# A gated recurrence with a convolutional gate on one core: tangents taken for each gate apart

## The chip, the cores and the metric

The kernel runs on one core of a Trainium2 chip. The core has a matrix engine (TensorE, PE in the profile, with its weight loads as PEld), a vector engine (VectorE, DVE), a scalar engine that evaluates functions from tables (ScalarE, ACT), a fourth engine for elementwise work (GpSimd, POOL), and a queue that issues transfers between the memory outside the core and the memory on it (SyncE, SP). The metric is the device time of one execution in microseconds (us). Where a time stands without more, it comes from the profiled execution.

## The reference: what is computed

There are three inputs of 4 sequences x 6336 steps x 256 channels in single precision: `x`, `r_gate` and `i_gate`. A gated linear recurrence runs along each sequence, and its output goes through a linear layer that is gated by a short causal convolution.

```
log_a = 8 * sigmoid(r_gate) * log(sigmoid(a_param))     # a_param: one number per channel
a     = exp(log_a)
u     = sqrt(max(1 - a*a, 1e-6)) * sigmoid(i_gate) * x
h[t]  = a[t] * h[t-1] + u[t]                            # along the sequence; y = h
gate  = sigmoid(sum over k of conv_w[k] * y[t-4+k])     # five taps, per channel, zeros ahead of the sequence
out   = (gate * (y @ w_val)) @ w_out                    # two 256 x 256 matrices
```

The steps `a*a`, the square root and the product with `i_gate` and `x` are independent of the recurrence, but the recurrence needs them; everything behind `y` needs the recurrence.

## The kernel before, in words

**Tiling.** The four sequences are laid end to end, 25344 rows. They are cut into 51 windows, 48 of 512 rows and 3 of 256 (windows 0, 1 and 50). The windows form 28 chunks: chunks 0, 1 and 27 are one short window each, chunks 2 and 26 one window of 512 each, and the 23 chunks between have two windows (chunk 3 is windows 3 and 4, chunk 4 windows 5 and 6, and so on). The chunks form 12 batches, mostly of three chunks; a batch shares one square root. Sigmoids are computed as tanh: sigmoid(z) = (1 + tanh(z/2)) / 2.

**Stages.** The kernel is a list of small operations. Their names are the words of a long string, `ORDER`, with the number of the window (w), chunk (c), half of the channels (h) or batch (b) that they work on:

- `lr.w`, `li.w`, `lx.w` (line 274): load r, i and x of a window, 512 KB for a window of 512 rows, issued by SP. `st.w` (line 493): store the output of a window, also issued by SP.
- `th.w` (line 289, ACT): the tanh of r and i of a window in one operation, 2048 elements in each partition for a window of 512 rows.
- `tr.c.h` (line 334, PE): transpose the tanh of r of a pair of chunks, so that time lies along the row. `ex.c.h` (line 350, ACT): the exponential, which gives a.
- `sq.c.h` (line 358, POOL): a*a; `sa.c.h` (line 366, ACT) is the same on ACT. `rt.b` (line 377, ACT): the square root for a batch. The exponential and the tanh are in one set of ACT's tables and the square root in another, so that a table load (line 509) stands ahead of rt and behind it.
- `pp.w` (line 297, POOL) adds one to the tanh of i, and `up.w` (line 309, POOL) multiplies with x, which gives u without its root. For a few windows `xp.w` (line 314, PE) and `uv.w` (line 323, DVE) do that in place of pp and up.
- `nt.c` (line 392, PE) transposes the root, `xg.c` (line 399, DVE) multiplies it into u, `xt.c` (line 408, PE) transposes u. `sc.c.h` (line 430, DVE): the recurrence, a scan.
- `cv.w` (line 442, PE): the convolution, as matmuls. `tg.w` (line 449, ACT): its tanh. `vl.w` (line 457, PE): y @ w_val. `gv.w` (line 462, DVE): gate times value. `ou.w` (line 472, PE): times w_out. `cd.w` (line 480, DVE) or `ca.w` (line 482, ACT): copy the result out of the matmul banks.

**What sets the order.** `ORDER` is written out in full. Each engine, and SP's queue, runs its own words in the order of the string, and waits for what it needs from another engine; a word that waits holds up every later word of its engine. The numbers behind an @ are the matmul banks that an operation uses.

**Rings.** Data between the stages lie in rings with a fixed number of places. r and i share one ring of 4 windows (`riring`). The tangents go to `tring`, with 3 windows of three planes each: the tanh of i is always in the middle plane, the tanh of r in the first or in the last in turn (`swapped`), so that one operation writes two planes that lie side by side:

Of the kernel before, what the change touches and what calls it, by code (L numbers as in the profile page):

```python
# [8 lines left out]
P = 128  # L9
CONV_K = 5  # L10
FP32 = mybir.dt.float32
BF16 = mybir.dt.bfloat16
# [12 lines left out]
NRI = 4  # L25
NX = 4
NTRI = 3
# [6 lines left out]
s_ident s_small s_kt s_diag li.2 lr.2 th.2 lr.3 lr.0 li.0 th.0 pp.0 tr.2.0@0 li.1 lr.1 tr.0.0@1 ex.2.0 th.1 lx.0 lx.2  # L34
li.3 up.0 tr.2.1@2 ex.2.1 tr.0.1@0 ex.0.0 tr.1.1@3 ex.1.1 tr.1.0@4 sq.1.1 ex.0.1 sq.0.1 lx.3 xp.3@0,1 lx.1 lr.6 th.3
sq.0.0 rt.0 lr.5 sq.2.0 pp.2 up.2 nt.0@5 xg.0 xt.0@2,3 li.5 th.5 sq.2.1 li.6 lr.4 uv.3 th.6 pp.6 pp.5 xp.1@5 sc.0.0
sc.0.1 cv.0@2,3 uv.1 li.4 th.4 tg.0 s_wl.1 ex.1.0 lx.4 li.7 tr.3.1@0,1 s_wl.0 lr.7 ex.3.1 lx.5 tr.3.0@2,3 ex.3.0
s_wl.3 lx.6 lx.7 pp.4 up.4 th.7 lr.9 rt.2 xp.7@2,3 li.8 uv.7 sa.4.0 sq.4.1 sq.3.1 sq.1.0 rt.1 nt.2@0 xg.2 nt.1@1 xg.1
s_wl.2 lr.8 li.10 lx.8 xt.2@2,3 xt.1@0,1 sc.1.1 li.9 lr.10 sq.3.0 rt.3 li.11 up.6 sc.1.0 lx.10 lr.11 sc.2.1 sc.2.0
up.5 th.8 lx.11 s_wcast th.10 lx.9 pp.10 up.10 lr.14 th.9 li.13 li.14 lr.13 xp.8@4,5 li.12 lr.12 uv.8 th.11 li.15  # L40
nt.3@0,1 xg.3 nt.4@6,7 pp.11 up.11 cv.1@2,3 tg.1 xg.4 xt.3@0,1 sc.3.1 vl.1@4,5 tr.5.0@6,7 ex.5.0 sq.5.0 tr.5.1@2,3
gv.1 ou.1.0@1 cd.1.0 st.1 lx.12 lr.15 ex.5.1 vl.0@4,5 xp.9@6,7 th.14 sq.5.1 cv.2@2,3 sc.3.0 th.13 uv.9 lx.13 xt.4@1,0
gv.0 ou.0.0@4 cd.0.0 st.0 sc.4.1 lx.15 cv.3@6,7 th.12 li.16 li.18 tr.7.1@4,5 tg.2 vl.2@2,3 gv.2 tg.3 ex.7.1 sq.6.1
sq.6.0 lx.14 pp.14 pp.12 up.12 tr.7.0@6,7 ex.7.0 sq.7.0 lx.16 cv.4@2,3 tg.4 th.15 ou.2.0@4,5 cd.2.0 sc.4.0 st.2 lr.18
lr.16 vl.3@6,7 xp.13@2,3 vl.4@4,5 gv.4 sq.7.1 rt.4 uv.13 th.16 sq.8.1 sq.8.0 pp.15 up.15 li.17 lr.17 up.14 ou.4.0@4,5
li.19 cv.5@0,1 lr.19 gv.3 cd.4.0 lx.17 tg.5 ou.3.0@6,7 lx.18 st.4 cd.3.0 st.3 nt.5@4,5 li.20 xg.5 pp.16 up.16 th.17
pp.17 lr.20 nt.7@6,7 xg.7 lx.19 li.21 nt.6@2,3 xg.6 th.18 pp.18 lr.21 xt.5@4,5 sc.5.1 up.17 vl.5@6,7 cv.6@0,1 tg.6
th.19 tr.9.1@2,3 ex.9.1 li.22 lr.22 up.18 sq.9.1 pp.19 gv.5 sc.5.0 tr.9.0@6,7 ex.9.0 lx.20 ou.5.0@0,1 cd.5.0 sq.10.1
xt.6@5,4 up.19 sc.6.1 cv.7@0,1 tg.7 cv.8@2,3 th.20 lr.24 tg.8 sc.6.0 vl.6@6,7 gv.6 xt.7@0,1 cv.9@4,5 ou.6.0@6,7 sc.7.0
th.21 tg.9 cd.6.0 vl.7@2,3 gv.7 vl.9@6,7 th.22 tr.11.0@0 sc.7.1 ou.7.0@2,3 vl.8@4,5 sq.9.0 tr.12.0@1 gv.9 ou.9.0@6,7  # L50
gv.8 ou.8.0@4,5 sq.10.0 st.5 cd.7.0 cd.9.0 lx.22 st.6 rt.5 lx.21 nt.8@6,7 lr.23 li.23 cd.8.0 nt.9@4,5 pp.22 pp.21
up.22 pp.20 up.20 up.21 xg.8 ex.12.0 xg.9 ex.11.0 li.24 st.7 st.9 li.25 lr.25 lx.23 lx.24 li.26 lr.26 th.23 xt.8@6,7
sc.8.0 sq.11.0 pp.23 sq.12.0 lr.27 li.27 cv.11@2,3 tg.11 cv.10@4,5 sc.8.1 cv.12@0,1 st.8 th.24 pp.24 tg.10 tg.12
vl.11@2,3 tr.11.1@6 ex.11.1 gv.11 vl.10@4,5 gv.10 th.25 xt.9@0,1 sc.9.0 tr.12.1@2 ex.12.1 ou.11.0@6,7 cd.11.0
ou.10.0@4,5 cd.10.0 cv.14@2,3 up.23 lx.25 lx.27 th.26 nt.10@6,7 sc.9.1 st.11 li.29 st.10 tg.14 tr.13.0@4,5 xg.10 up.24
sq.11.1 th.27 ex.13.0 tr.13.1@2,3 vl.12@0,1 gv.12 sq.12.1 li.30 lr.30 lx.26 pp.25 pp.27 sq.13.0 xt.10@6,7 sc.10.1
ex.13.1 sq.13.1 up.27 sq.14.0 pp.26 up.25 lr.28 cv.13@4,5 tg.13 vl.13@0,1 gv.13 li.28 vl.14@2,3 gv.14 ou.12.0@4,5
# [42 lines left out]
def kernel(  # L100
# [82 lines left out]
    with tc.manual_schedule():  # L183
# [357 lines left out]
```

## Time and profile before

| | |
|---|---|
| median of 3 runs | 301.36 us (300.97 to 302.71) |
| the profiled execution | 300.32 us, its span 298.5 us |
| ACT busy | 278.8 us (93%), 197 instructions |
| DVE busy | 247.6 us (83%), 206 instructions |
| PE busy | 246.4 us (83%), 2509 matmuls |
| POOL busy | 232.8 us (78%), 155 instructions |
| moved by transfers | 104.75 MB, 351 GB/s over the span |
| granted PE clock | 0.977 of full speed |

The span is the time from the first to the last instruction on the core; the device time is a little longer. The profile gives each engine's busy time; the same in 40 slices of the span, where a digit is the busy share in tenths; groups of instructions by line; who waited for whom; and the instructions in order of time, with their start, their duration and, in brackets, the idle time ahead of them and what ended it.

### The profile page before, as it was taken

To read this page: it belongs to the slowest core of one execution; us is meant where nothing else is said; L and a number is where in the kernel's file an instruction comes from. 1 tells how busy PE (TensorE), PEld (TensorE's weight loads), DVE (VectorE), ACT (ScalarE), POOL (GpSimd) and SP (SyncE) were. 2 spreads that over 40 slices of the span, in tenths; PEclk is the share of its full clock that TensorE was granted. 3 is DMA by queue.
4 is the path that set the end of the run, shared out by engine and by line. 5 is a ranking of instruction groups with operands and counts; after the bars stand their busy time and mean duration, and the time that the engine had idled before them with its cause. 6 is when DMAs were issued, how large, how long until landed. Compare 5 with 4: busy or idle time off the path is not lost.

```text
span 298.5 us, 6286 instructions
## 1 busy us (share of the span) xinstructions
PE 246.4 (83%) x2509; PEld 167.8 (56%) x2509; DVE 247.6 (83%) x206; ACT 278.8 (93%) x197; POOL 232.8 (78%) x155
## 2 busy tenths in 40 slices
PE   0374577897888598989898899998979999899993
PEld 0134255454556466757664758567647675666662
DVE  2030288849999889999999999999999899899993
ACT  6799999999999999999999999999999999969863
POOL 1478958989999899899999879998995996255300
PEclk9997599999999979999999999999999999999999
DMA  6999999999999999999999998999999977726046
GB/s 252 408 408 385 379 411 407 406 414 406 337 379 370 419 416 415 411 406 321 417 411 375 388 417 335 396 353 361 349 409 419 408 278 270 273 116 248 29 186 246
DMA packets 29995, 104.75 MB, mean 351 GB/s; under 512 B 3335, under 2 KB 3854, under 8 KB 29966
## 3 DMA queue, kind: packets, MB, share of 16 engines
q1 hardware_dynamic: 29952, 104.35, 90.5%
q8 instruction: 19, 0.31, 0.4%
q14 instruction: 10, 0.08, 0.1%
q10 hardware_dynamic: 14, 0.01, 0.0%
HBM read 78.39 MB, written 25.95 MB: 350 GB/s over the span
## 4 chain that ended last, share of the span: by engine, by line
ACT 31%; PE 23%; DVE 13%; issue 13%; DMA 12%; POOL 5%; SPq 1%; ACTq 0%; DVEq 0%; POOLq 0%
ACT tring L289 10%; ACT aring L350 8%; DMA riring<-in_r_gate_dram 7%; DVE yring L430 7%; PE banks L442 5%; ACT tgring L449 5%; PE banks L457 5%; ACT ering L377 4%; PE banks L472 4%; PE banks L392 3%; DMA riring<-in_i_gate_dram 3%; DVE tgring L462 3%; DVE oring L480 2%; DMA xring<-in_x_dram 2%; ACT L509 2%
## 5 line engine op out<-in xcount | busy, mean ns | idle before, releaser
L430 DVE TENSOR_TENSOR_SCAN yring<-aring,yring,banks 128x1024 bf16<-128x1024 f32 (+5 forms) x54 | 106.2, 1988 | 0.9 <-PE banks L408 0.6
L358 POOL TENSOR_TENSOR ering<-aring 128x1024 f32<-128x1024 f32 (+2 forms) x54 | 91.5, 1713 | 9.7 <-ACT aring L350 9.7
L309 POOL TENSOR_TENSOR uring<-tring,xring 128x1024 bf16<-128x1024 bf16 (+1 forms) x45 | 94.6, 2113 | 4.9 <-DMA xring<-in_x_dram 3.5
L289 ACT ACTIVATE tring<-riring 128x2048 bf16<-128x2048 f32 (+1 forms) x51 | 93.8, 1867 | 4.1 <-DMA riring<-in_i_gate_dram 1.9
L297 POOL TENSOR_SCALAR tring<-tring 128x1024 bf16<-128x1024 bf16 (+1 forms) x45 | 45.8, 1026 | 30.5 <-ACT tring L289 30.4
L442 PE MATMUL banks<-yring,diag 64*64 64x512 bf16 (+7 forms) x1080 | 61.9, 361 | 4.6 <-ACT aring L350 1.6
L462 DVE SCALAR_TENSOR_TENSOR tgring<-tgring,banks 128x1024 bf16<-128x1024 bf16 (+1 forms) x51 | 58.9, 1178 | 5.5 <-PE banks L457 4.4
L472 PE MATMUL banks<-wo,tgring 128*128 128x256 bf16 x396 | 51.4, 274 | 4.7 <-DVE tgring L462 3.5
L350 ACT ACTIVATE aring<-banks,khf 128x2048 f32<-128x2048 bf16 (+3 forms) x38 | 54.1, 1474 | 0.5 <-PE banks L334 0.4
L449 ACT ACTIVATE tgring<-banks 128x1024 bf16<-128x1024 f32 (+1 forms) x51 | 50.4, 1009 | 3.4 <-PE banks L442 3.3
L457 PE MATMUL banks<-yring,wv 128*128 128x512 bf16 (+4 forms) x216 | 49.4, 361 | 5.0 <-DVE oring L480 2.2
L472 PEld LDWEIGHTS <-tgring 128*128 128x128 bf16 x396 | 41.0, 114 | 15.7 <-DVE tgring L462 9.6
L442 PEld LDWEIGHTS <-diag 64*64 64x64 bf16 x1080 | 30.3, 106 | 28.8 <-issue 13.6
L377 ACT ACTIVATE ering<-ering 128x4096 bf16<-128x4096 f32 (+5 forms) x15 | 44.9, 3019 | 0.1
L399 DVE TENSOR_TENSOR uring<-banks,uring 128x2048 bf16<-128x2048 bf16 (+2 forms) x28 | 29.8, 1095 | 18.2 <-PE banks L392 17.9
L480 DVE COPY oring<-banks 128x1024 f32<-128x1024 f32 (+1 forms) x35 | 40.6, 1181 | 4.8 <-ACT aring L350 2.4
L334 PE MATMUL banks<-ident_b,tring 128*128 128x128 bf16 x396 | 29.0, 227 | 12.2 <-ACT tring L289 10.4
L334 PEld LDWEIGHTS <-tring 128*128 128x128 bf16 x396 | 25.1, 101 | 17.7 <-ACT tring L289 11.7
L457 PEld LDWEIGHTS <-wv 128*128 128x128 bf16 x216 | 19.7, 97 | 26.3 <-issue 12.4
L392 PE MATMUL banks<-ident,ering 128*128 128x128 f32 x198 | 28.8, 296 | 6.8 <-DVE oring L480 2.6
L392 PEld LDWEIGHTS banks<-ident,ering 128*128 128x128 f32 x198 | 25.9, 208 | 13.5 <-ACT ering L377 7.7
L408 PE MATMUL banks<-ident,uring 128*128 128x128 f32 x198 | 27.5, 282 | 2.6 <-DVE uring L399 2.5
(36 smaller groups left out, 113.1 us busy)
## 6 DMA issues: line engine op xcount, KB each, us to landing
riring<-in_i_gate_dram SPq DMA_DIRECT2D x48, 512.0 KB, 8.2
riring<-in_r_gate_dram SPq DMA_DIRECT2D x48, 512.0 KB, 8.3
xring<-in_x_dram SPq DMA_DIRECT2D x48, 512.0 KB, 8.0
out_dram<-oring SPq DMA_DIRECT2D x48, 512.0 KB, 5.7
riring<-in_r_gate_dram SPq DMA_DIRECT2D x3, 256.0 KB, 6.3
riring<-in_i_gate_dram SPq DMA_DIRECT2D x3, 256.0 KB, 6.5
xring<-in_x_dram SPq DMA_DIRECT2D x3, 256.0 KB, 5.3
out_dram<-oring SPq DMA_DIRECT2D x3, 256.0 KB, 7.3
```

The source lines that it names most:

```text
L289: nc.scalar.activation(out=tring[:, w % NTRI, a:a + 2, 0:J, :], in_=riring[:, w % NRI, :, 0:J, :], func=ACT.Tanh, scale=0.5)
L309: nc.gpsimd.tensor_tensor(out=u, in0=t1, in1=xt, op=ALU.mult)
L350: nc.scalar.activation(out=dst, in_=src, func=ACT.Exp, scale=khf[:, h:h + 1], bias=khf[:, h:h + 1])
L358: nc.gpsimd.tensor_tensor(out=e, in0=a, in1=a, op=ALU.mult)
L377: nc.scalar.activation(out=ering[:].bitcast(BF16)[:, 4 * o:4 * o + 2 * n], in_=ering[:, 2 * o:2 * o + 2 * n], func=ACT.Sqrt, scale=-0.25, ...
L392: nc.tensor.transpose(out=bank[:, k:k + P], in_=ering[:, e + q:e + wins[w] // 2:nq], identity=ident[:])
L430: nc.vector.tensor_tensor_scan(out=yring[:, h, col:col + o1 - o0], data0=aring[:, h, a_at[c] + o0:a_at[c] + o1], data1=xT[:, o0:o1], initi ...
L442: nc.tensor.matmul(out=gp[oh * 64:oh * 64 + 64, h, a:b], lhsT=diag[half * 64:half * 64 + 64, h, k, :], rhs=yring[half * 64:half * 64 + 64, ...
L449: nc.scalar.activation(out=tgring[:, w % NTG, :, 0:wins[w]], in_=live.pop(("gp", w))[:, :, 0:wins[w]], func=ACT.Tanh, scale=0.5)
L457: nc.tensor.matmul(out=val[:, m, a:b], lhsT=wv[:, hk, m * P:(m + 1) * P], rhs=yring[:, hk, col:col + b - a], start=(hk == 0), stop=(hk == ...
L462: nc.vector.scalar_tensor_tensor(out=tgring[:, w % NTG, :, 0:wins[w]], in0=tgring[:, w % NTG, :, 0:wins[w]], scalar=1.0, in1=live.pop(("va ...
L472: nc.tensor.matmul(out=ops[:, j * D:(j + 1) * D], lhsT=gv[:, hk, j:wins[w]:J], rhs=wo[:, hk, :], start=(hk == 0), stop=(hk == H - 1))
```

## The change

The one tangent operation per window, for both gates, becomes two operations per chunk, one for r (`ta.c`) and one for i (`tb.c`). Each takes all windows of the chunk: for a chunk of two windows of 512 rows it has 2048 elements in each partition, as the operation before had. r and i get rings of their own (`rring` and `iring`, 4 windows each), and so do their tangents (`taring`, 6 windows, and `tbring`, 4 windows). A window's place is (w + 1) modulo the length of the ring, so that the two windows of a chunk lie side by side.

`ORDER` is a new string: every word has another place, on every engine and in SP's queue, and other banks. Windows 1, 4, 6 and 10 now go by xp and uv, where it was windows 1, 3, 7, 8, 9 and 13; 17 results are copied by ca and 34 by cd, where it was 16 and 35; the squares on ACT are sa.9.1 and sa.26.0, where they were sa.4.0 and sa.27.0. Chunks, batches, pairs of chunks and all other rings are as before.

```diff
@@
-NTRI = 3
+NII = 4
+NTR = 6
+NTI = 4
@@
-s_ident s_small s_kt s_diag li.2 lr.2 th.2 lr.3 lr.0 li.0 th.0 pp.0 tr.2.0@0 li.1 lr.1 tr.0.0@1 ex.2.0 th.1 lx.0 lx.2
...
+s_ident s_small s_kt s_diag lr.1 ta.1 tr.1.1@0 lr.0 ta.0 tr.1.0@1 tr.0.0@2 lr.2 ta.2 tr.2.0@3 ex.1.0 li.0 tb.0 li.2
+lr.3 lr.4 ex.1.1 sq.1.1 lr.5 tb.2 ta.3 tr.0.1@1 ex.0.0 lr.6 sq.0.0 ex.0.1 pp.0 ta.4 li.1 tb.1 sq.0.1 ex.2.0 tr.2.1@4
...
@@
-        riring = rings.tile([P, NRI, 2, 4, D], FP32, name="riring")
+        rring = rings.tile([P, NRI, 4, D], FP32, name="rring")
+        iring = rings.tile([P, NII, 4, D], FP32, name="iring")
         xring = rings.tile([P, NX, 4, D], FP32, name="xring")
-        tring = rings.tile([P, NTRI, 3, 4, D], BF16, name="tring")
+        taring = rings.tile([P, NTR, 4, D], BF16, name="taring")
+        tbring = rings.tile([P, NTI, 4, D], BF16, name="tbring")
@@
-        def swapped(w):
-
-            return (w // NTRI) % 2
+        def place(w, n):
+            return (w + 1) % n
@@
-                dst = riring[:, w % NRI, "ri".index(which) ^ swapped(w), 0:J, :]
+                ring = rring if which == "r" else iring
+                dst = ring[:, place(w, NRI if which == "r" else NII), 0:J, :]
@@
-        def op_th(w):
-            J = wins[w] // P
-            a = swapped(w)
-            nc.scalar.activation(out=tring[:, w % NTRI, a:a + 2, 0:J, :], in_=riring[:, w % NRI, :, 0:J, :],
-                                 func=ACT.Tanh, scale=0.5)
+        def tangent(c, dst, nd, src, ns):
+            w, k = cwins[c][0], len(cwins[c])
+            J, a, t = wins[w] // P, place(w, ns), place(w, nd)
+            nc.scalar.activation(out=dst[:, t:t + k, 0:J, :], in_=src[:, a:a + k, 0:J, :], func=ACT.Tanh, scale=0.5)
+
+        def op_ta(c):
+            tangent(c, taring, NTR, rring, NRI)
+
+        def op_tb(c):
+            tangent(c, tbring, NTI, iring, NII)
@@
-                                        in_=tring[:, w % NTRI, 2 * swapped(w), j, h * P:(h + 1) * P],
+                                        in_=taring[:, place(w, NTR), j, h * P:(h + 1) * P],
@@
-        table, have = {"th": EXP, "tg": EXP, "ex": EXP, "rt": SQRT}, EXP
+        table, have = {"ta": EXP, "tb": EXP, "tg": EXP, "ex": EXP, "rt": SQRT}, EXP
```

pp, up and uv read the tanh of i from `tbring` in the same way.

More of the change, by code (lines that the diff above doesn't have):

```diff
@@ L94 @@
[L94 to L95 removed]
+s_ident s_small s_kt s_diag lr.1 ta.1 tr.1.1@0 lr.0 ta.0 tr.1.0@1 tr.0.0@2 lr.2 ta.2 tr.2.0@3 ex.1.0 li.0 tb.0 li.2
+lr.3 lr.4 ex.1.1 sq.1.1 lr.5 tb.2 ta.3 tr.0.1@1 ex.0.0 lr.6 sq.0.0 ex.0.1 pp.0 ta.4 li.1 tb.1 sq.0.1 ex.2.0 tr.2.1@4
+li.4 lx.0 li.3 ex.2.1 up.0 tb.3 lx.2 pp.2 sq.2.1 up.2 tr.3.0@0,1 ex.3.0 pp.3 sq.4.0 tr.3.1@2,3 ex.3.1 lx.1 xp.1@4
+sq.3.1 sq.3.0 sq.4.1 lr.10 lr.9 ta.6 lr.7 lr.8 ta.5 sq.2.0 li.5 li.6 uv.1 tr.5.1@2,3 tb.4 ex.5.1 lx.4 xp.4@0,1 sq.1.0
@@ new lines @@
+tr.21.1@0 ou.27.0@6,7 cd.27.0 ex.21.1 pp.38 sq.21.1 tr.21.0@2 ex.21.0 ta.24 lr.44 sq.21.0 pp.37 xt.17@1,3 sc.17.0
+cv.29@4,5 tg.29 cv.30@6,7 sc.17.1 tb.21 tr.22.0@2 xt.18@0,1 ex.22.0 tg.30 ou.28.0@4,5 st.24 cd.28.0 tr.22.1@3
+vl.29@4,5 sc.18.1 st.27 vl.30@6,7 lx.39 gv.30 gv.29 lx.37 st.26 cv.31@1,2 ta.23 sc.18.0 ex.22.1 nt.19@6,7 tg.31
+vl.31@4,5 gv.31 xg.19 lx.40 li.44 lx.38 ou.30.0@2,3 ou.31.0@4,5 cd.30.0 sq.22.0 sq.22.1 rt.9 ou.29.0@0,1 ca.31.0
+cd.29.0 lr.47 xt.19@6,7 sc.19.1 cv.33@2,3 sc.19.0 lr.49 li.42 st.28 li.41 li.43 lr.48 up.37 pp.39 up.39 pp.40 up.38
@@ new lines @@
+cv.32@0,1 vl.33@4,5 tg.33 gv.33 tg.32 vl.32@2,3 tr.23.0@0,1 tb.22 gv.32 up.40 nt.21@6,7 xg.21 nt.20@4,5 xg.20 ex.23.0
+ou.33.0@2,3 lx.41 st.29 cd.33.0 ta.25 ou.32.0@6,7 cd.32.0 cv.34@0,1 lx.43 pp.41 tb.23 lx.42 li.45 tg.34 xt.20@4,5
+sc.20.0 tr.23.1@2,3 ex.23.1 cv.35@6,7 tg.35 sc.20.1 cv.36@0,1 tg.36 lx.44 li.46 st.32 tr.25.0@2 ex.25.0 vl.35@3,4
+gv.35 vl.36@6,7 gv.36 st.30 tr.25.1@5 ex.25.1 pp.42 sq.23.0 up.41 pp.44 up.42 st.31 tb.24 ta.26 vl.34@0,1 gv.34
+xt.21@2,3 sc.21.1 st.33 cv.38@6,7 ou.34.0@0,1 ca.34.0 st.34 li.48 li.50 lx.45 lr.50 cv.37@4,5 tg.37 sc.21.0
@@ L96 @@
+sc.26.1 sc.26.0 cv.49@2,3 ca.46.0 tg.49 st.46 gv.47 gv.48 xt.27@4,5 ou.47.0@0,1 ca.47.0 st.47 vl.49@6,7 sc.27.1
+ou.48.0@2,3 ca.48.0 sc.27.0 cv.50@0,1 st.48 gv.49 tg.50 ou.49.0@6,7 ca.49.0 st.49 vl.50@2,3 gv.50 ou.50.0@2 ca.50.0
+st.50
 """
@@ L283, in op_lx @@
             load(w, "x")
-        def op_th(w):
-            J = wins[w] // P
-            a = swapped(w)
-            nc.scalar.activation(out=tring[:, w % NTRI, a:a + 2, 0:J, :], in_=riring[:, w % NRI, :, 0:J, :],
-                                 func=ACT.Tanh, scale=0.5)
+        def tangent(c, dst, nd, src, ns):
[6 more added lines that the diff above has]
+            tangent(c, tbring, NTI, iring, NII)
         def gate_of_input(w):
-            return tring[:, w % NTRI, 1, 0:wins[w] // P, :].rearrange("p j d -> p (j d)")
+            return tbring[:, place(w, NTI), 0:wins[w] // P, :].rearrange("p j d -> p (j d)")
         def op_pp(w):
@@ L304, in u_args @@
             return (uring[:, (w + 1) % NU, 0:wins[w] // (2 * P)].rearrange("p q d two -> p q two d"),
-                    by_pair(tring[:, w % NTRI, 1], w), by_pair(xring[:, w % NX], w))
+                    by_pair(tbring[:, place(w, NTI)], w), by_pair(xring[:, w % NX], w))
         def op_up(w):
```

108 lines of the change are left out of this document (46 added, 62 removed).

## The prediction

> **What bounds the kernel now.** First the page: busy times and slices.
>
> ```profile
> span 298.5 us, 6286 instructions
> PE 246.4 (83%) x2509; PEld 167.8 (56%) x2509; DVE 247.6 (83%) x206; ACT 278.8 (93%) x197; POOL 232.8 (78%) x155
> ...
> ACT  6799999999999999999999999999999999969863
> ...
> DMA  6999999999999999999999998999999977726046
> GB/s 252 408 408 385 379 411 407 406 414 406 337 379 370 419 416 415 411 406 321 417 411 375 388 417 335 396 353 361 349 409 419 408 278 270 273 116 248 29 186 246
> DMA packets 29995, 104.75 MB, mean 351 GB/s; under 512 B 3335, under 2 KB 3854, under 8 KB 29966
> ```
>
> ScalarE (ACT) is full from about 15 us on; the last six slices are something else. So the kernel has a head, a stage where ACT is the bound, and a tail. The stretches by engine give their borders and their limits:
>
> ```profile
> 120.00:160.00 40.00, 36.52 (x404) 25.52 (x403) 39.15 (x28) 39.92 (x27) 38.49 (x23) 1.00 1.02 389
> ...
> 260.00:270.00 10.00, 10.00 (x106) 6.54 (x99) 9.95 (x8) 6.98 (x8) 5.38 (x4) 1.00 0.35 142
> ...
> 254.88:294.95 40.07, 38.88 (x404) 26.21 (x404) 36.78 (x31) 30.38 (x31) 12.82 (x10) 1.00 0.46 173
> ```
>
> (Columns: stretch, PE, PEld, DVE, ACT, POOL, clock, DMA share, GB/s.) From 120 to 160 us ACT is idle for 0.08 of 40 us, DVE for 0.85, and the DMA share is full too. In the third row, from the end of the square root of batch 10 (rt.10) to the end of the last matmul, TensorE (PE) works 38.88 of 40.07 us and ACT only 30.38: the tail belongs to PE. The two borders, and the rows that release them:
>
> ```profile
> 245.35 3.74 POOL L358 TENSOR_TENSOR ering<-aring 128x1024 f32<-128x1024 f32 x2 [0.27 <-ACT aring L350]
> ...
> 248.21 1.28 ACT L509 ACT_TABLE_LOAD   x1
> ...
> 249.51 5.33 ACT L377 ACTIVATE ering<-ering 128x6144 bf16<-128x6144 f32 x1
> ...
> 254.89 2.19 PE L392 MATMUL banks<-ident,ering 128*128 128x128 f32 x16 [0.89 <-ACT ering L377]
> ...
> 294.31 0.61 PE L472 MATMUL banks<-wo,tgring 128*128 128x256 bf16 x4 [0.88 <-DVE tgring L462]
> ```
>
> rt.10 ends at 249.51 + 5.33 = 254.84; nt.23 follows on PE at once. So span = (ACT's work up to the end of rt.10 + ACT's idle time before it) + PE's work from nt.23 on + 2 us of gaps. The change is costed on this path. Note also that the last squares of the batch end at 249.09, 0.4 us before rt.10 starts: POOL is nearly as tight as ACT.
>
> **The change, part by part.** The prices of ACT's operations, from starts that follow each other without a gap:
>
> ```profile
> 137.26 5.52 ACT L289 ACTIVATE tring<-riring 128x2048 bf16<-128x2048 f32 x3
> 142.67 1.02 ACT L482 COPY oring<-banks 128x1024 f32<-128x1024 f32 x1
> 143.56 1.96 ACT L449 ACTIVATE tgring<-banks 128x1024 bf16<-128x1024 f32 x2
> 145.38 1.94 ACT L289 ACTIVATE tring<-riring 128x2048 bf16<-128x2048 f32 x1
> ...
> 10.85 1.04 ACT L289 ACTIVATE tring<-riring 128x1024 bf16<-128x1024 f32 x1
> 11.79 2.13 ACT L350 ACTIVATE aring<-banks,khf 128x512 f32<-128x512 bf16 x4
> ...
> L509 ACT ACT_TABLE_LOAD x20 | 25.7, 1283 | 0.4
> ...
> L449 ACT ACTIVATE tgring<-banks 128x512 bf16<-128x512 f32 x3 | 1.8, 584 | 0.5 <-PE banks L442 0.5
> ```
>
> A tangent of 2048 elements takes (142.67 - 137.26) / 3 = 1.80 us of ACT's time, a copy 0.89, a tg 0.91, a tangent of 1024 elements 0.94, a table load 1.28. A tangent of 512 elements isn't in the trace: between half of 0.94 (0.47) and the tg of 512 (0.58 with its overlap); I take 0.49, the tg's less the 0.1 by which neighbours overlap.
>
> 1. *Tangents split by gate.* Before: 48 of 2048 and 3 of 1024 elements. After: 23 chunks of two windows give 46 of 2048, two of one window 4 of 1024, three short ones 6 of 512. Whole kernel: -2 x 1.80 + 0.94 + 6 x 0.49 = +0.3 us. Elements are the same; only five starts are added.
> 2. *Table switches.* Walking both orders by ACT's words, exp and sqrt sets change 20 times before and 18 after (rt.0 now stands with rt.1 to rt.3): -2 x 1.28 = -2.6. One more ca: +0.9. A square on ACT of 512 in place of 256: +0.2. ACT's whole work: -1.2 us.
> 3. *The new order, on ACT up to rt.10.* Counted in both orders, what differs is: tangents of 2048 47 to 45 (-3.60), of 1024 2 to 3 (+0.94), of 512 0 to 4 (+1.96), tg 40 to 39 (-0.91), ca 6 to 3 (-2.67), table loads 17 to 15 (-2.57). Sum -6.8 us: r runs ahead, i and the copies are put off.
> 4. *The new order, on PE from nt.23.* One more cv, one more ou, two more vl stand behind it. The chain of waits prices them:
>
> ```profile
> 285.42 0.87 PE banks L472 x8
> 286.29 0.86 PE banks L457 x4
> 287.15 1.21 PE banks L442 x19
> ```
>
> 1.21 + 0.87 + 2 x 0.86 = +3.8 us. So 3 and 4 together: -3.0. ACT's put-off work (-1.2 + 6.8 = 5.6 us more behind rt.10) makes 30.38 + 5.6 = 36.0 in a tail of some 43.9, DVE's (one gv and one scan more, two cd fewer, about +1.1) 37.9: both below PE's 42.7, so they cost nothing there; were PE's cover gone, DVE's 1.1 would count.
> 5. *POOL and DVE.* Two windows fewer go by xp and uv, two more by pp and up.
>
> ```profile
> L323 DVE SCALAR_TENSOR_TENSOR uring<-tring,banks 128x512 bf16<-128x512 bf16 x11 | 7.6, 732 | 13.1 <-PE banks L314 12.8 <-ACT tring L289 0.3
> ...
> L309 POOL TENSOR_TENSOR uring<-tring,xring 128x1024 bf16<-128x1024 bf16 x43 | 92.3, 2157 | 4.5 <-DMA xring<-in_x_dram 3.2
> ...
> L297 POOL TENSOR_SCALAR tring<-tring 128x1024 bf16<-128x1024 bf16 x43 | 44.5, 1045 | 21.8 <-ACT tring L289 21.6
> ```
>
> POOL gains 2 x (1.05 + 2.16) = 6.4 us, DVE loses 4 x 0.73 = 2.9 and a cd. Where POOL's sits decides: ahead of the last square of rt.6 both orders have 21 pp, 19 up, 27 sq; ahead of that of rt.10 the new one has two pp and one up fewer (-4.3). The additions stand behind rt.10, where POOL works 12.82 of 40 us. Cost 0. The cover: between the ends of rt.10 and rt.11 ACT has about 22 us of work in the new order at the prices of this part, and behind nt.26 PE has about 13 (three cv, three vl, four ou, and the short windows); 22 + 13 stands against a tail of 43.9, so squares of the last batch that came 9 us late would begin to cost.
> 6. *The head and the loads.* ACT's waits there now:
>
> ```profile
> 3.46 1.28 ACT L230 ACT_TABLE_LOAD   x1
> ...
> 5.58 1.91 ACT L289 ACTIVATE tring<-riring 128x2048 bf16<-128x2048 f32 x1 [0.83 <-DMA riring<-in_r_gate_dram]
> ...
> 9.22 1.06 ACT L289 ACTIVATE tring<-riring 128x1024 bf16<-128x1024 f32 x1 [1.73 <-DMA riring<-in_i_gate_dram]
> ...
> 46.95 1.91 ACT L289 ACTIVATE tring<-riring 128x2048 bf16<-128x2048 f32 x1 [0.57 <-DMA riring<-in_r_gate_dram]
> ...
> riring<-in_r_gate_dram SPq DMA_DIRECT2D x48, 512.0 KB, 8.3
> ```
>
> The SP queue issues the same transfers in another order, the stores among them. For each tangent I set the bytes issued up to its load, at 0.405 MB/us (the page's slices show 406 to 419 GB/s where loads run freely), against ACT's work ahead of it, summed at the prices above from 4.74 us, where the table load above ends. Tightest before: li.4, 7.9 MB, 19.4 against 20.0 us, 0.6 in hand. After: lr.14, 14.4 MB, 35.6 against 37.1, 1.5 in hand. So 0.9 us less waiting. Ends: the two first waits go whole (-2.6), or one like the worst comes anew (+1.7). I take -0.9, as the margins are of one kind.
>
> Sum: -6.8 + 3.8 - 0.9 = -3.9 us against the profiled execution of 300.32 us (span 298.5 and 1.8 around it): 296.4. The median of the runs, 301.36, is 1.04 above that execution: **297.5**.
>
> A price that only a page states: the Trainium skill, "ScalarE: Activation LUTs", section "What ACT_TABLE_LOAD costs", puts a switch at about 2.66 us, the 1.28 of the load and a drain of 1.38. By it two switches fewer would give 2.8 more, 294.7. In the rows above rt.10 starts 0.02 us after its load ends, so this trace shows no drain behind it; the load alone is what I count.
>
> **The rivals.**
> *POOL sets the pace.*
>
> ```profile
> POOL tring L297 <- ACT tring L289: 30.4, 11, 8.7
> ...
> 124.61 3.84 POOL L358 TENSOR_TENSOR ering<-aring 128x1024 f32<-128x1024 f32 x2 [0.84 <-ACT aring L350]
> ...
> 128.69 5.43 ACT L377 ACTIVATE ering<-ering 128x2048 bf16<-128x2048 f32 x2
> ```
>
> For: the squares of rt.6 end at 128.45, 0.24 us before it. If POOL's 30.4 us of waits for tangents don't shrink, rt.10 moves only by POOL's -4.3, not ACT's -6.8 - 0.9: with PE's +3.8 that is -0.5, 300.9. Against: r tangents come earlier, so the squares do. Chance 0.14.
> *Loads in pairs (the other side).* A slot of r or i is now free only when its chunk's tangent has read both windows. Between that and the next tangent on the same slots, ACT's order leaves least, past the first 15 us, at ta.9 (6.6 us), ta.6 (7.7) and tb.7 (8.5). A load lands after a median of 8.3 us, the second of a pair 1.3 later (512 KB at 408 GB/s): 9.6. If it holds there, ACT waits 3.0 + 1.9 + 1.1 = 6.0 us in the first 60 us: 297.5 + 6.0 = 303.5. It decides from 3.9 us of such waits. Against: the old order has places of 7.3 and 8.1 us too, and its rows show waits of 0.57 at most after the first 10 us; the 8.3 is that of a full queue. Chance 0.19.
> *The transfers are the floor.* The DMA share is full to 240 us; then nothing moves earlier: 301.4. Against: slices of 419 GB/s beside a mean of 350. Chance 0.06. The Trainium skill, "DMA: Bandwidth & Descriptors", section "Specifications", gives some 358 GB/s of HBM for a core; 104.75 MB would by that take 293 us, hardly less than the span forecast. The trace disagrees: 26 of its 40 slices run above 360 GB/s.
>
> **How the numbers follow.** Forecast 0.61, with its own range from its ends: -3.0 - 2.6, and the 1.2 us of PE's gaps in the tail gone too (-6.8), to -3.0 + 1.7 (-1.3): 294.6 to 300.1. A change under 0.5% (1.5 us) can't be told from none in this kernel. Faster: 0.61. Same: 0.14 + 0.06 = 0.20. Slower: 0.19. The range, 294.5 to 303.0, takes in the forecast's own and both cases of no change, and leaves out the upper half of the paired loads.
>
> **What would show it.** Right: rt.10 ends near 247 us, ACT's idle time between 50 us and there below 1 us; PE full from nt.23 over about 44 us; 18 table loads of 1.28; POOL some 239 us busy; the first 50 us with under 3.5 us of ACT's waits on loads. Wrong: waits of ACT on the loads of r or i at ta.6, ta.9 or tb.7 above 3.9 us together; or squares that end after ACT has loaded the sqrt table, at rt.6 first; or PE in the tail waiting for scans or for u, which I take to be ready.

## The result, and the profile after

The changed kernel takes 297.74 us (median of 4 runs, 295.08 to 299.15), the kernel before beside it 301.72 (300.97 to 302.71): a ratio of 0.9857, 95% interval 0.9817 to 0.9896, or 4.0 us less. The forecast was 297.5. Run once more on another chip (the run r_again below) it took 297.63 against 301.73, ratio 0.9892 [0.9836, 0.9948]. The ratios are those on record; the quotients of the medians differ from them by up to 0.003. Differences in us are differences of medians, and a profile is of one execution.

The page of the changed kernel (its profiled execution took 299.15 us), with the lines that answer to those of before: busy times, the slices of ACT, of PE's granted clock and of DMA, and the bytes moved.

```profile
span 297.1 us, 6249 instructions
...
PE 244.5 (82%) x2501; PEld 168.2 (57%) x2501; DVE 244.1 (82%) x201; ACT 277.9 (94%) x201; POOL 238.2 (80%) x159
...
ACT  5899989999999999999999899999999999987954
...
PEclk9999979999999999999997999999999999999999
DMA  6999999999999999999999999988999759973516
...
DMA packets 29994, 104.74 MB, mean 353 GB/s; under 512 B 3335, under 2 KB 3854, under 8 KB 29966
```

ACT's work is 0.9 us less (1.2 were counted), POOL's 238.2 (239 were counted), the bytes are the same to 0.01 MB. The span of this execution is only 1.4 us shorter than before, 297.1 against 298.5, though the medians differ by 4.0. A second profile, of r_again, has a span of 294.7 us and took 296.82. The stretches of the three profiles say where the two differ. First the kernel before: from the start to the end of rt.3, to the end of rt.10, and to the end of the last copy. (Columns as in the prediction: stretch, its length, busy time of PE, PEld, DVE, ACT and POOL, clock, DMA share, GB/s.)

```profile
0.00:39.56 39.56, 17.58 (x97) 9.97 (x97) 8.44 (x20) 34.29 (x29) 25.73 (x28) 0.87 0.97 369
39.56:254.84 215.28, 189.96 (x2008) 131.58 (x2008) 202.38 (x157) 213.55 (x136) 194.21 (x118) 0.99 0.99 383
254.84:295.54 40.70, 38.88 (x404) 26.21 (x404) 36.82 (x31) 30.99 (x32) 12.82 (x10) 1.00 0.46 177
```

Then the changed kernel, the same three stretches of its first profile:

```profile
0.00:38.90 38.90, 17.96 (x101) 11.08 (x101) 6.26 (x16) 34.14 (x30) 24.97 (x26) 1.00 0.96 366
38.90:249.23 210.33, 183.44 (x1960) 128.61 (x1960) 199.06 (x156) 207.07 (x134) 194.56 (x121) 0.98 0.98 378
249.23:294.10 44.87, 43.08 (x440) 28.56 (x440) 38.79 (x31) 36.66 (x40) 18.69 (x15) 1.00 0.61 233
```

And those of its second profile:

```profile
0.00:38.75 38.75, 17.01 (x101) 10.86 (x101) 6.36 (x16) 34.20 (x30) 25.02 (x26) 0.87 0.96 366
38.75:246.85 208.10, 180.91 (x1960) 126.42 (x1960) 198.78 (x156) 206.53 (x133) 194.54 (x121) 1.00 0.98 383
246.85:291.72 44.87, 43.08 (x440) 28.56 (x440) 38.77 (x31) 36.65 (x40) 18.70 (x15) 1.00 0.61 232
```

By the second profile the head is 0.81 us shorter, the middle 7.18 us shorter and the tail 4.17 us longer: -3.82, where the prediction's sum was -3.9. rt.10 ends at 246.85 us. The first profile differs mainly in the middle, by 2.2 us. Some 0.8 of them arise between the starts of rt.6 and rt.7 (29.17 us there, 28.33 in the second profile), where ACT waits for a load of i, and 1.1 between those of rt.7 and rt.10 (88.64 and 87.51). The timeline of the first profile shows places of both:

```profile
151.13 1.91 ACT L293 ACTIVATE tbring<-iring 128x2048 bf16<-128x2048 f32 x1 [0.60 <-DMA iring<-in_i_gate_dram]
...
155.27 5.33 ACT L386 ACTIVATE ering<-ering 128x6144 bf16<-128x6144 f32 x1
...
160.65 3.48 PE L401 MATMUL banks<-ident,ering 128*128 128x128 f32 x16 [2.46 <-ACT ering L386]
...
167.68 2.06 ACT L359 ACTIVATE aring<-banks,khf 128x2048 f32<-128x2048 bf16 x1 [0.57 <-PE banks L343]
```

The second profile has no wait at the place of the first line. The same transposes there:

```profile
159.40 2.19 PE L401 MATMUL banks<-ident,ering 128*128 128x128 f32 x16 [1.64 <-ACT ering L386]
```

PE takes 3.48 us in the first profile in place of 2.19, and ACT, which waits for the transposes behind it, loses 0.32 and 0.57. In the stretch from 160 to 165 us the granted clock of the two profiles is

```profile
160.00:165.00 5.00, 4.35 (x33) 4.29 (x34) 3.86 (x3) 4.70 (x4) 2.87 (x3) 0.66 1.03 418
```

in the first and

```profile
160.00:165.00 5.00, 5.00 (x59) 4.54 (x58) 5.00 (x5) 4.99 (x4) 2.84 (x3) 1.00 1.03 419
```

in the second. The second has its own slow stretch (0.50 from 23 to 33 us), in the head, where PE has time to spare. So its mean clock is the lower one, 0.979 against 0.988, and its span the shorter. In what follows the second profile stands for the changed kernel.

### The profile page after: what moved, and what is told of

Its sections match the earlier page's. It is cut to its first block, busy times and chain, and to the rows that moved or that the text cites. A ratio compares the mean times of both kernels' runs of the same rounds, so it can differ in the third digit from the quotient of the medians.

```text
span 297.1 us, 6249 instructions
## 1 busy us (share of the span) xinstructions
PE 244.5 (82%) x2501; PEld 168.2 (57%) x2501; DVE 244.1 (82%) x201; ACT 277.9 (94%) x201; POOL 238.2 (80%) x159
## 4 chain that ended last, share of the span: by engine, by line
ACT 27%; PE 25%; DMA 20%; DVE 13%; issue 7%; POOL 5%; SPq 1%; ACTq 0%; DVEq 0%; POOLq 0%
DMA xring<-in_x_dram 9%; DVE yring L439 7%; PE banks L451 6%; ACT ering L386 6%; PE banks L466 6%; PE banks L481 6%; ACT aring L359 5%; ACT taring L293 5%; ACT tbring L293 4%; DMA rring<-in_r_gate_dram 4%; ACT tgring L458 4%; DMA out_dram<-oring 3%; PE banks L401 3%; DVE tgring L471 3%; DMA iring<-in_i_gate_dram 3%
## 5 line engine op out<-in xcount | busy, mean ns | idle before, releaser
L318 POOL TENSOR_TENSOR uring<-tbring,xring 128x1024 bf16<-128x1024 bf16 (+1 forms) x47 | 98.6, 2112 | 9.2 <-DMA xring<-in_x_dram 7.3
L451 PE MATMUL banks<-yring,diag 64*64 64x512 bf16 (+7 forms) x1080 | 63.1, 365 | 2.6 <-ACT tgring L458 0.9
L306 POOL TENSOR_SCALAR tbring<-tbring 128x1024 bf16<-128x1024 bf16 (+1 forms) x47 | 47.9, 1028 | 10.8 <-ACT tbring L293 10.8
L466 PE MATMUL banks<-yring,wv 128*128 128x512 bf16 (+4 forms) x216 | 50.4, 361 | 5.1 <-ACT tgring L458 3.1
L481 PEld LDWEIGHTS <-tgring 128*128 128x128 bf16 x396 | 41.5, 114 | 17.8 <-DVE tgring L471 10.2
L293 ACT ACTIVATE taring<-rring 128x2048 bf16<-128x2048 f32 (+2 forms) x28 | 47.7, 1716 | 3.2 <-DMA rring<-in_r_gate_dram 3.2
L293 ACT ACTIVATE tbring<-iring 128x2048 bf16<-128x2048 f32 (+2 forms) x28 | 47.6, 1713 | 0.9 <-DMA iring<-in_i_gate_dram 0.8
L343 PE MATMUL banks<-ident_b,taring 128*128 128x128 bf16 x396 | 31.2, 233 | 16.2 <-ACT taring L293 14.4
L451 PEld LDWEIGHTS <-diag 64*64 64x64 bf16 x1080 | 29.7, 107 | 26.0 <-issue 10.2
L489 DVE COPY oring<-banks 128x1024 f32<-128x1024 f32 (+1 forms) x34 | 39.5, 1181 | 1.7 <-PE banks L481 0.9
L401 PE MATMUL banks<-ident,ering 128*128 128x128 f32 x198 | 30.3, 300 | 12.3 <-ACT ering L386 6.7
L343 PEld LDWEIGHTS <-taring 128*128 128x128 bf16 x396 | 26.9, 105 | 23.7 <-ACT taring L293 17.0
```

What stands on the lines that cost most here:

```text
L293: nc.scalar.activation(out=dst[:, t:t + k, 0:J, :], in_=src[:, a:a + k, 0:J, :], func=ACT.Tanh, scale=0.5)
L318: nc.gpsimd.tensor_tensor(out=u, in0=t1, in1=xt, op=ALU.mult)
L401: nc.tensor.transpose(out=bank[:, k:k + P], in_=ering[:, e + q:e + wins[w] // 2:nq], identity=ident[:])
L451: nc.tensor.matmul(out=gp[oh * 64:oh * 64 + 64, h, a:b], lhsT=diag[half * 64:half * 64 + 64, h, k, :], rhs=yring[half * 64:half * 64 + 64, ...
L466: nc.tensor.matmul(out=val[:, m, a:b], lhsT=wv[:, hk, m * P:(m + 1) * P], rhs=yring[:, hk, col:col + b - a], start=(hk == 0), stop=(hk == ...
L481: nc.tensor.matmul(out=ops[:, j * D:(j + 1) * D], lhsT=gv[:, hk, j:wins[w]:J], rhs=wo[:, hk, :], start=(hk == 0), stop=(hk == H - 1))
```

## The experiments

The theory was the prediction's: ACT's work sets the time up to rt.10, PE's behind it; POOL, DVE and the transfers lie beside. The rivals were its rivals. The runs stand beside the kernel before, 301.4 to 301.7 us on each chip; the changed kernel is 297.7.

**The splitting alone (a_split_old).** The kernel before, with each of its tangents cut into one for r and one for i: 51 more starts.

```diff
-            nc.scalar.activation(out=tring[:, w % NTRI, a:a + 2, 0:J, :], in_=riring[:, w % NRI, :, 0:J, :], ...)
+            for g in range(2):
+                nc.scalar.activation(out=tring[:, w % NTRI, a + g, 0:J, :], in_=riring[:, w % NRI, g, 0:J, :], ...)
```

> The kernel before with its order and rings unchanged, but each tangent cut in two: one operation for r, one for i, per window. The elements are the same, 51 starts more. Theory (ACT's work ahead of rt.10 sets its place): each start costs the 0.09 us by which a tangent of 2048 elements (1.80) is less than two of 1024 (0.94 each, 1.88) to 0.1 us, 48 of them ahead of rt.10, so +4 to +5 us, 305.5 to 306.5. Rival (the split by gate is itself the gain, because transposes of r can start before the tangent of i is done): no loss, or up to 2 us faster. Rival (POOL or the transfers set the pace): within 1 us of the kernel before.

Measured: 304.51 us, ratio 1.0102 [1.0031, 1.0174], +3.1. That is 0.06 us for a start, less than the 0.09 expected, but the interval (0.9 to 5.2 us) holds both, and ACT's busy time in the profile rose by 4.7 us (283.5 against 278.8), 0.09 for a start. So the split by itself gains nothing. Taken per window it costs 3.1 us; taken per chunk it adds five starts, 0.3 to 0.5 us.

**Two table loads, with and without the rings (b_rt0_old, c_rt0_new).** b is the kernel before with rt.0 next to rt.2, and chunk 0's nt, xg, xt, sc, cv and tg moved behind it; c is the changed kernel with rt.0 back in its early place.

```diff
 # b_rt0_old: ORDER of the kernel before
-sq.0.0 rt.0 lr.5 ... th.7 lr.9 rt.2 ... rt.3 li.11
+sq.0.0 lr.5 ... th.7 lr.9 rt.0 rt.2 ... rt.3 tg.0 li.11
 # c_rt0_new: ORDER of the changed kernel
-ex.2.1 up.0 ... s_wl.1 lx.3 rt.0 lx.5
+ex.2.1 rt.0 up.0 ... s_wl.1 lx.3 lx.5
```

> The kernel before, with the square root of batch 0 moved to stand with those of batches 1 to 3, and what hangs on it (nt.0, xg.0, xt.0, sc.0, cv.0, tg.0) moved behind it: 18 table loads in place of 20, nothing else. Theory: 2 x 1.28 = 2.6 us less of ACT ahead of rt.10, the same PE work behind it: -2.6, about 299. DVE does chunk 0's 2 us later, which costs nothing as DVE is idle there. Rival (a switch costs 2.66 with a drain): -5.3, about 296. Rival (POOL or the transfers set the pace from 60 us on, ACT is merely full): no change, 301.5.

> The changed kernel with the square root of batch 0 alone, ahead of the tangents of chunks 3 and 4 of gate i: 20 table loads in place of 18. Theory: +2.6 us, about 300.3. Rival (drain): +5.3, about 303. Rival (POOL or transfers set the pace): 0 to +1, about 298.

Measured: c 300.03 us, ratio 0.9941 [0.9908, 0.9975], 2.3 above the changed kernel, as expected. b missed: 304.15 us, ratio 1.0066 [1.0021, 1.0111], slower by 2.7 instead of faster by 2.6. The timelines of ACT at th.5, the first of the kernel before and then of b:

```profile
19.57 3.71 ACT L289 ACTIVATE tring<-riring 128x2048 bf16<-128x2048 f32 x2 [0.54 <-POOL uring L309]
```

```profile
19.38 3.71 ACT L289 ACTIVATE tring<-riring 128x2048 bf16<-128x2048 f32 x2 [3.81 <-POOL uring L309]
...
55.53 3.71 ACT L289 ACTIVATE tring<-riring 128x2048 bf16<-128x2048 f32 x2 [1.44 <-DMA riring<-in_i_gate_dram]
```

th.5 starts at 19.38 in place of 19.57: the time of the two loads turned into a wait for a place of `tring`, which holds three windows and is freed by POOL's up. That takes the gain away. The 2.7 us of loss beyond it are only in part explained: later ACT waits 1.44 us for a load of i, and up to rt.10 it waits 1.8 us for PE's transposes ahead of exponentials, where the kernel before shows no such wait. So joining rt.0 did not pay in the old rings and order, and did in the new ones, where r's tangents have six places. That it is the places that make the difference was not tried apart from the order.

**The price of a load (d_loads).** Five pairs of table loads more, in front of ta.9, ta.12, ta.15, ta.18 and ta.21.

```diff
+        def op_xs():
+            nc.scalar.preload_act_table_set("sqrt_and_others")
+            nc.scalar.preload_act_table_set("exp_and_others")
-... li.11 ta.9 sc.3.1 ...
+... li.11 xs ta.9 sc.3.1 ...
```

> The changed kernel with five extra pairs of table loads (sqrt and back), one ahead of the r tangents of chunks 9, 12, 15, 18 and 21: ten loads more, all ahead of rt.10. Theory: ACT is the bound there and a load costs 1.28: +12.8 us, about 310.5. Rival (a load and a drain, 2.66): +26.6, about 324. Rival (POOL, DVE or the transfers are the bound and ACT has room): below +8.

Measured: 313.49 us, ratio 1.0410 [1.0355, 1.0465], +15.8 for ten loads. In its groups of ACT:

```profile
L359 ACT ACTIVATE aring<-banks,khf 128x2048 f32<-128x2048 bf16 (+3 forms) x38 | 54.8, 1466 | 5.8 <-PE banks L343 4.5 <-DVE yring L439 1.3
...
L506 ACT ACT_TABLE_LOAD x5 | 6.4, 1283 | 0.1
```

A load is still 1.28 us and the gap ahead of the loads is 0.1 in all. The rest (15.8 - 12.8 = 3.0) goes with longer waits of the exponentials on PE and DVE: 5.8 us here, 1.6 in the second profile of the changed kernel. How much of these waits comes from the loads can't be read off: this profile is of the slowest of the four executions (316.48 us), at a mean PE clock of 0.949, and the exponentials wait for PE's transposes. By the Trainium skill, "ScalarE: Activation LUTs", section "What ACT_TABLE_LOAD costs", a switch would be some 2.66 us with a drain of 1.38; ten of them would by that, as an estimate, be 26.6. This case's runs give 1.2 for each of two (c) and 1.6 for each of ten (d), and in d part of that is ACT's waits for other engines.

**POOL relieved, and the transfers relieved (e_pp, f_st).** The changed kernel with pp on 128 of 1024 columns, and with half of each window's output stored.

```diff
 # e_pp
-nc.gpsimd.tensor_scalar(out=t, in0=t, ...)
+nc.gpsimd.tensor_scalar(out=t[:, 0:128], in0=t[:, 0:128], ...)
 # f_st
-    of[...].rearrange("(p j) d -> p j d", p=P), oring[:, w % NOSB, 0:J, :]
+    of[...].rearrange("(p j) d -> p j d", p=P)[:, 0:J // 2], oring[:, w % NOSB, 0:J // 2, :]
```

> The changed kernel with POOL's addition of one to the tangent of i done on an eighth of the elements only (the rest is left out): POOL's work falls by about 47 x 0.75 = 35 us, its order and waits stay. Theory: POOL is hidden, its squares end 0.06 us and more ahead of the roots: 0 to -1 us, about 297. Rival (POOL sets the pace): -3 us or more.

> The changed kernel storing only half of each output window (the other half is left out): 13 of 104.7 MB less. Theory: transfers are no floor, they are only just in time: 0 to -1.5 us, about 297. Rival (the transfers are the floor): the stage up to 240 us shortens with the bytes, by 12% of it at most; -5 us or more.

Measured: e 296.49 us, ratio 0.9860 [0.9799, 0.9921]; f 296.48 us, ratio 0.9823 [0.9789, 0.9857]. Both ratios' intervals overlap those of the changed kernel. The middle of e:

```profile
38.66:246.40 207.74, 180.93 (x1960) 126.38 (x1960) 198.79 (x156) 206.52 (x134) 166.18 (x121) 1.00 0.98 383
```

POOL works 28.4 us less (166.18 against 194.54) and the middle is 0.36 us shorter. 13 MB fewer in f gave 1.2 us by the medians, which the intervals can't tell from nothing. Neither sets the pace.

**The tail (g_ou).** The changed kernel without half of the last product's matmuls in windows 38 to 50.

```diff
-                for hk in range(H):
+                n = 1 if w >= 38 else H
+                for hk in range(n):
```

> The changed kernel with half of the matmuls of the last product left out for windows 38 to 50, the 13 that stand behind nt.23: 12 x 0.44 + 0.25 = 5.5 us less of PE in the tail. Theory: PE is the bound of the tail (42.9 of 44.1 us); with 37.4 left, DVE's 38.8 takes over: -4 us, about 293.7. Rival (a chain through scans and roots sets the tail, with PE only full beside it): 0 to -1 us.

Measured: 296.46 us, ratio 0.9810 [0.9769, 0.9852]; 1.3 below the changed kernel, where 4 were expected. The interval overlaps that of the changed kernel, so the median alone does not show a gain; the profile shows where it is. The tail in its profile, from the end of rt.10 to that of the last copy:

```profile
246.83:289.38 42.55, 38.43 (x390) 23.68 (x390) 38.46 (x31) 36.10 (x40) 18.68 (x15) 1.00 0.64 248
```

PE's work fell by 4.65 us (43.08 to 38.43), the tail by 2.3 (44.87 to 42.55). PE is then no fuller than DVE, 38.46, and neither fills the 42.55: beyond 2.3 us, PE's work alone no longer sets the end. Which of the waits between the engines does was not taken apart.

**Work moved between ACT, DVE and POOL (j_cd, p_ca, m_uv), beside the changed kernel again (r_again).** j gives three copies ahead of rt.10 from ACT to DVE, p three from DVE to ACT; m gives windows 6 and 10 from PE and DVE (xp, uv) to POOL (pp, up).

```diff
 # j_cd
-ca.22.0 ... ca.31.0 ... ca.34.0
+cd.22.0 ... cd.31.0 ... cd.34.0
 # p_ca
-cd.11.0 ... cd.18.0 ... cd.27.0
+ca.11.0 ... ca.18.0 ... ca.27.0
 # m_uv
-xp.6@4,5 ... uv.6 ... xp.10@4,5 ... uv.10
+pp.6 up.6 ... pp.10 up.10
```

> The changed kernel with the three results copied by ACT ahead of rt.10 (windows 22, 31 and 34) copied by DVE instead. Theory: 3 x 0.89 = 2.7 us less of ACT ahead of rt.10; DVE takes 3 x 1.18 = 3.5 more in a stage where it is busy for 98%: if ACT alone sets rt.10, -2.7, about 295; if DVE is as tight as ACT there, the gain is lost in later scans, and the time stays or rises by up to 1 us. I expect -1, about 296.7.

> The changed kernel with three copies ahead of rt.10 (cd.11, cd.18, cd.27) on ACT in place of DVE: ACT +3 x 0.89 = +2.7 us ahead of rt.10, DVE about -3.5. ACT alone sets the pace there: +2.7 against the changed kernel, 300.4. DVE sets the pace with it, in turn: what DVE gains is given back in part, 0 to +1.5, 297.7 to 299.2. DVE alone sets it: faster, 296.

> The changed kernel with windows 6 and 10 by pp and up (POOL) in place of xp and uv (PE and DVE): POOL +6.4 us, DVE -2.9, PE -3.5, all ahead of rt.6. My step 5 (none of the three sets the pace there): 297.7, no change. DVE as tight as ACT: 1 to 2 us faster. POOL as tight: rt.6 follows its last square by 0.06 us in the changed kernel, so up to +6, 300 to 303.

> The changed kernel unaltered, beside the next two on the same chip. Theory: 297.7, a ratio of 0.986, as before; in a profile without the slow stretch of the PE clock at 160 us the part from the end of rt.3 to the end of rt.10 takes 207.7 to 208.5 us, as it did with the smaller pp, the halved stores and the halved last product, in place of the 210.3 of the disturbed profile. Rival (the 210.3 belong to the order): 210 or more again at a clock of 1.00.

Measured: r_again 297.63 us, with a middle of 208.10. So the 210.3 do not belong to the order; the late load of i and the slow clock near 160 us account for most of the difference. j 299.77 us, ratio 0.9970 [0.9937, 1.0002], +2.0 against an expected -1. p 301.82 us, ratio 1.0020 [0.9993, 1.0047], +4.1. m 301.22 us, ratio 0.9985 [0.9949, 1.0021], +3.5. The middles, of j, of p and of m, each from a profile of its own:

```profile
38.26:250.57 212.31, 183.06 (x1971) 128.53 (x1968) 203.38 (x163) 204.87 (x130) 195.30 (x121) 0.99 0.97 374
```

```profile
38.85:251.80 212.95, 182.42 (x1960) 127.64 (x1960) 196.02 (x153) 209.69 (x136) 194.58 (x121) 0.99 0.98 374
```

```profile
38.91:251.56 212.65, 183.13 (x1956) 128.99 (x1956) 197.16 (x152) 207.52 (x133) 200.77 (x124) 0.97 0.97 374
```

All three are 4.2 to 4.9 us longer than 208.10, but only 2.0 to 2.6 longer than the 210.33 of the first profile, and that is the nearer comparison: like the first profile, each of the three has a clock of 0.50 for some 3.4 us near 160 us. The medians say +2.0, +4.1 and +3.5, whichever engine got the work. In j ACT has 1.7 us less to do than in r_again and waits more: the group of the exponentials, in j and then in r_again, stands idle 5.5 us in place of 1.6. Of that, 2.0 us are waits on DVE's scans, where both profiles of the changed kernel have 0.2.

```profile
L359 ACT ACTIVATE aring<-banks,khf 128x2048 f32<-128x2048 bf16 (+3 forms) x38 | 55.0, 1467 | 5.5 <-PE banks L343 3.4 <-DVE yring L439 2.0
```

```profile
L359 ACT ACTIVATE aring<-banks,khf 128x2048 f32<-128x2048 bf16 (+3 forms) x38 | 54.8, 1471 | 1.6 <-PE banks L343 1.4
```

In p ACT works 3.2 us more than in r_again and 2.6 more than in the first profile, and its middle is 2.6 longer than the first profile's: what was expected if ACT alone sets the pace, +2.7. The median's +4.1 is more than that, and the excess was not taken apart. A give-back by DVE does not show in either. In m the last square ahead of rt.6, and rt.6:

```profile
126.44 1.90 POOL L367 TENSOR_TENSOR ering<-aring 128x1024 f32<-128x1024 f32 x1
...
128.15 5.42 ACT L386 ACTIVATE ering<-ering 128x2048 bf16<-128x2048 f32 x2
```

against r_again:

```profile
123.78 1.88 POOL L367 TENSOR_TENSOR ering<-aring 128x1024 f32<-128x1024 f32 x1
...
125.68 5.42 ACT L386 ACTIVATE ering<-ering 128x2048 bf16<-128x2048 f32 x2
```

The square is 2.7 us later and rt.6 2.5, but rt.6 does not wait for it: in m it starts at 128.15, before the square ends at 126.44 + 1.90 = 128.34. rt.6 is two operations, the first for chunk 11 and the second for chunks 12 and 13, and only the second reads this square, which is of chunk 13. The line of rt.6 in r_again and then in m:

```profile
L386 ACT ACTIVATE ering<-ering x2: 1916/2761/3606, 125.7 to 127.5; 128x2048 bf16<-128x2048 f32 x1, 128x4096 bf16<-128x4096 f32 x1
```

```profile
L386 ACT ACTIVATE ering<-ering x2: 1914/2760/3606, 128.2 to 130.0; 128x2048 bf16<-128x2048 f32 x1, 128x4096 bf16<-128x4096 f32 x1
```

The second operation starts at 127.5 and 130.0, 1.8 and 1.7 us behind the end of the square. What ACT loses in m on its way to rt.6 are other waits:

```profile
71.97 1.91 ACT L293 ACTIVATE tbring<-iring 128x2048 bf16<-128x2048 f32 x1 [0.65 <-POOL uring L318]
...
101.40 1.21 ACT L359 ACTIVATE aring<-banks,khf 128x1024 f32<-128x1024 bf16 x1 [0.65 <-DVE yring L439]
```

Of the 6.4 us that POOL was given, 0.65 thus show as a wait for POOL. 0.65 is a wait for a scan (0.16 in r_again), and 0.84 in all are waits for PE, whose clock falls to 0.50 twice on this stretch. How much of these two follows from POOL's work is not shown. From the start of rt.6 to that of rt.10 m takes 118.1 us, the first profile of the changed kernel 117.8 and r_again 115.8, so the loss there is not m's own. None of these variants beats the changed kernel.

## Why the prediction was right, by its steps

The time, the sign and the path were right: 297.5 forecast, 297.74 and 297.63 measured. The executions of the changed kernel spread over 4.5 us, so that the sum meets the medians to 0.2 us is partly luck; that the two large terms have the right sign and size, on the engines named for them, is not. Term by term:

1. *Tangents split.* +0.3 was counted for five starts, about 0.06 each. a_split_old gives 0.06 for a start by the medians and 0.09 by ACT's busy time. The tangent of 512 elements, bounded at 0.47 to 0.58 and taken at 0.49 behind an overlap of 0.1, has a row now, in the groups of ACT:

```profile
L293 ACT ACTIVATE tbring<-iring 128x512 bf16<-128x512 f32 x3 | 1.9, 620 | 0.0
```

0.62 in place of 0.59, six times: 0.2 us more.

2. *Table switches.* 18 loads of 1.28 were forecast:

```profile
L518 ACT ACT_TABLE_LOAD x18 | 23.1, 1283 | 0.3
```

The worth of the two, 2.6, is confirmed in the changed kernel (c, +2.3). It is not worth that everywhere: in the old rings and order the time of the two loads goes into another wait (b). The step priced a load rightly and did not say that the price is had only where nothing else holds ACT.

3. *ACT up to rt.10*, -6.8. ACT's busy time in the first two stretches goes from 34.29 + 213.55 = 247.84 to 34.20 + 206.53 = 240.73: -7.1.

4. *PE from nt.23*, +3.8. The tail is 4.17 longer, PE's work in it 43.08 - 38.88 = 4.2. The size was right. That PE sets the tail's end is only half so: in g 4.65 us less of PE's work gave 2.3. The step took DVE to be covered by the 4.8 us between the two busy times (42.7 and 37.9); the cover that could be used was about half of that. DVE's own work there was counted too low: it rose by 1.95 us (36.82 to 38.77) in place of 1.1, as two scan operations of 2.33 us more stand behind rt.10, where one was counted, and three copies fewer. The 2 us of gaps in the prediction's equation are 4.8 us in both kernels (298.5 - 254.84 - 38.88 and 294.7 - 246.85 - 43.08), 3.0 of them behind the last copy; they drop out of the difference.

5. *POOL and DVE, cost 0.* The sum was right, the reason too narrow. They cost nothing in a change that lowers DVE's work in the middle (202.38 to 198.78) and leaves POOL's as it was (194.21, 194.54). j and m show that there was not much room: three copies more on DVE cost 2 us, with 2.0 us of waits for scans, and 6.4 us more on POOL cost 3.5 by the medians, of which the profile shows 0.65 as a wait for POOL.

6. *Head and loads*, -0.9. ACT's idle time up to rt.10, the stretches less the busy time, goes from 254.84 - 247.84 = 7.0 to 246.85 - 240.73 = 6.1: -0.9. By the first profile it would be +1.0 (249.23 - 34.14 - 207.07 = 8.0), so one profile does not settle a term of this size. And in the second it isn't the loads, as the step had it. The waits of ACT up to rt.10, before and then in r_again:

```profile
ACT tring L289 <- DMA riring<-in_i_gate_dram: 1.9, 2, 1.7
ACT tring L289 <- DMA riring<-in_r_gate_dram: 1.4, 2, 0.8
...
ACT tring L289 <- POOL uring L309: 0.5, 1, 0.5
ACT tgring L449 <- PE banks L442: 0.5, 1, 0.5
```

```profile
ACT taring L293 <- DMA rring<-in_r_gate_dram: 3.2, 3, 1.6
...
ACT tbring L293 <- DMA iring<-in_i_gate_dram: 0.2, 1, 0.2
ACT tgring L458 <- PE banks L451: 0.2, 1, 0.2
ACT aring L359 <- DVE yring L439: 0.2, 1, 0.2
```

The loads' waits stay: 3.3 before, 3.4 after. What went is the wait on POOL for a place of `tring` and some of PE's, 0.6 us net; the rest of the 0.9 is in gaps that the profile names no releaser for. The size was met by luck; the place was wrong.

**The rivals.** *POOL sets the pace*: not in this kernel (e); how much room POOL has left m does not settle. What spoke for it was misread in part: the square of the kernel before that ends at 128.45 is read by the second operation of rt.6, which starts at 130.5, so it had 2.1 us in hand and not 0.24. *Loads in pairs*: ACT's waits on loads in r_again are four, 3.4 us in all, under the 3.5 of the prediction's list, and from 50 us to rt.10 ACT waits 0.4 us for anything that the profile names. None of the waits is at ta.6, ta.9 or tb.7, so a load in these places comes faster than 8.3 + 1.3 us after its slot is free. *The transfers are the floor*: they are not, by f.

**The list of what would show it** came out as written in the second profile. The first misses it in two points, for the late load and the slow clock named above: rt.10 ends at 249.24 in place of 247, and ACT's idle time between 50 us and the start of rt.10 is 2.2 us (0.8 in the second). The squares of rt.6, listed as the first to come late, came in time: the last ends at 123.78 + 1.88 = 125.66, 1.8 us ahead of the operation that reads it.

## What to carry to other kernels

Where one engine is full in one stage and another in the next, count each engine's work on its own side of the border; here that gave 3.9 us against a measured 4.0, while the totals (ACT 0.9 us less, DVE 3.5 less, POOL 5.4 more) would have told little. A term of nothing is a margin, not a fact: in a kernel that is this evenly loaded three more copies cost 2 us on DVE and 4 us on ACT. A margin between two times is one only if the later operation reads what the earlier one writes. And a saving that is real in one arrangement (a table load) can be worth nothing in another, where a ring's place is what the engine waits for.

## What the runs showed of the hardware

PE's granted clock falls to 0.50 for stretches of 3.4 to 10.2 us (a window of 5 us that holds only a part of one reads up to 0.81), and not at the same places in each execution of a kernel: the changed kernel has falls at 41 and 160 us in one profile and from 23 to 33 us in the other. The 3.4 us ahead of a fall and the fall itself, in the first profile and then in the second:

```profile
157.00:160.40 3.40, 1.18 (x20) 0.40 (x20) 3.40 (x3) 3.40 (x1) 3.39 (x3) 0.99 1.03 413
160.40:163.80 3.40, 3.15 (x15) 3.16 (x16) 2.53 (x2) 3.37 (x4) 1.27 (x2) 0.50 1.02 417
```

```profile
19.70:23.10 3.40, 1.10 (x2) 0.30 (x2) 0.73 (x1) 3.40 (x3) 3.40 (x3) 1.00 1.02 410
23.10:33.30 10.20, 5.41 (x20) 2.81 (x20) 0.00 (x0) 9.93 (x7) 10.20 (x8) 0.50 1.03 408
```

PE works 1.2 and 1.1 us of the 3.4 ahead of them, and in all 13 profiles of this case no fall comes behind 3.4 us in which PE worked more than 1.8. That the idle time of PE is the cause, and why the same order has a fall in one execution and not in the next, wasn't tried. In the stage where PE's transposes feed ACT the fall at 160 us goes with 1.1 us more, in the head with nothing (38.75 us with it, 38.90 without); so the mean clock of a run doesn't tell its time. Eight executions of the changed kernel spread from 295.08 to 299.62 us, and two at a clock of 1.00 took 295.08 and 297.43, so the clock is not the whole of it.

A table load of 1.28 us is followed by the next activation within 0.02 us where that waits for nothing else, and the loads added in d have 0.1 us of gaps ahead of them in all: no drain is to be seen in the rows.
